# A second MLP's first layer by seven products of quadrants, on one core of a Trainium2 chip

## The chip, the cores and the metric

The kernel runs as one program on one core of one Trainium2 chip. The metric is the device time of one execution in microseconds (us). TensorE does the matrix products, VectorE (DVE in the rows) and ScalarE (ACT) the work between them; SyncE (SP) issues every DMA from one queue.

## What is computed

```python
def _moe_ref(x, w_gate, w_val, w_out, rms_g):
    rms = np.sqrt(np.mean(x * x, axis=-1, keepdims=True) + 1e-06)
    xn = x / rms * rms_g
    g = xn @ w_gate
    silu = g * (1.0 / (1.0 + np.exp(-g)))
    val = xn @ w_val
    return silu * val @ w_out

def _moe2_ref(x, w_in, w_out):
    h = x @ w_in
    g = np.maximum(0.01 * h, h)
    return g @ w_out

def reference(**kwargs):
    attn_out = _attn_ref(...)            # B, H, S, D = 4, 8, 544, 64
    x = attn_out.transpose(0, 2, 1, 3).reshape(B * S, H * D)
    x = _moe_ref(x=x, **moe_kwargs)      # 512 -> 1536 -> 512
    return _moe2_ref(x=x, **moe2_kwargs) # 512 -> 2048 -> 512
```

There are 2176 tokens (4 batches of 512 local and 32 global rows) of 512 columns. The weights of both MLPs come as 64-bit floats.

## The kernel before

Attention and the first MLP (`mlp1`) are not changed, apart from the jobs that `mlp1` carries along for the second MLP. The first MLP leaves its result y, transposed, in DRAM (`y_dram`, four chunks of 128 columns by 2176 tokens).

Every product is made of three matmuls (`mm3`, L69 to L72): each operand is split into a high part in the reduced 32-bit format and the rest (`split`: a cast on ScalarE at L75, a subtraction on VectorE at L78), and high x high, low x high and high x low are added up in PSUM. Each of these matmuls loads its own 128 x 128 weights.

The second MLP goes over token blocks of 512, 512, 512, 384 and 256 (`BLOCKS2`). For each block there are 16 steps f (NF2 = 16 groups of 128 hidden columns). A step makes `ph`, 128 hidden columns by n tokens, out of 4 chunks of the inner dimension, so 12 matmuls of n columns (L820); then leaky ReLU on ScalarE (`tl`, L822) and a split (`h2h`, `h2l`); and then, for the step before, the second layer (`out2_step`, L809): for every 128 tokens 3 matmuls of 512 columns into the banks `o`. PSUM has 4 banks for `ph` and 4 for `o`.

A 64-bit weight tile (128 x 512, 512 KB; `w64b`) becomes a 32-bit one in `weights2`: a DMA, `narrow` (one ScalarE instruction at L99 into `nc_b`, two of VectorE at L101 and L103, `nr_b` and `wfb`), and a split into `w0h`, `w0l` (first layer) or `w1h`, `w1l` (second). There are 32 such tiles, and all 64 halves stay in SBUF for the rest of the program. `ahead` makes 12 of them and the first block's split y while the first MLP's last blocks run; the other 20 are made during block 0 of the second MLP, with three buffers for `w64b`.

The order on every engine is fixed when the program is built: a list scheduler goes by the program's order and by when it expects each instruction's inputs and buffers. On the chip every engine takes its rows strictly in that order, SP's DMA issues included.

Of the kernel before, what the change touches and what calls it, by code (L numbers as in the profile page):

```python
# [20 lines left out]


@with_exitstack
def tile_window_global_attention_two_mlps(
# [600 lines left out]
    def rows_in(i, c, tmp, tag):  # L632

        pool, n, c0 = pre2[0], BLOCKS2[i], sum(BLOCKS2[:i])
        if c == 0:
# [4 lines left out]

    def weights2(f, k, pool, tmp, tag, bufs, wf_bufs):

        r = tmp.tile([P, DM, 2], U32, tag=tag, bufs=bufs, name=f"w64b{k}_{f}")
# [1 line left out]
        wf = tmp.tile([P, DM], F32, tag="wf", bufs=wf_bufs, name=f"wfb{k}_{f}")
        narrow(tmp, wf, r, f"b{k}_{f}")
        w2_s[f, k] = [pool.tile([P, DM], F32R, tag=f"w{k}{y}{f}", name=f"w{k}{y}{f}") for y in "hl"]
        split(w2_s[f, k][0], w2_s[f, k][1], wf)

    def ahead():  # L650

        ph_at.close()
# [1 line left out]
        jobs = []
        for f in range(6):
            for k in range(2):
                jobs.append(lambda f=f, k=k: weights2(f, k, pre2[0], mp, f"w64{k}", W64[k], 7))
        for c in range(KC):
            jobs.insert(2 * (c + 1) - 1, lambda c=c: rows_in(0, c, mp, "sq"))
# [140 lines left out]
    c0 = 0  # L800
    for i, n in enumerate(BLOCKS2):
        if i not in ys2:
            for c in range(KC):
                rows_in(i, c, wp2, "yf")
        ys = ys2.pop(i)
        op = [pools[0].tile([P, DM], F32, tag="y", bufs=4, name=f"o{t}_{i}") for t in range(n // P)]
        pend = None

        def out2_step(f, hs):  # L809
            for t in range(n // P):  # L810
                mm3(op[t], [h[:, t * P:(t + 1) * P] for h in hs], w2_s[f, 1], f == 0, f == NF2 - 1)

        for f in range(NF2):
            if i == 0:
                for k in range(2):
                    if (f, k) not in w2_s:
                        weights2(f, k, wp2, wp2, "w64", 3, 2)
            pp = bank(f"ph{i}_{f}")
            for c in range(KC):
                mm3(pp[:, 0:n], [w[:, c * P:(c + 1) * P] for w in w2_s[f, 0]], [y[:, c, 0:n] for y in ys], c == 0, c == KC - 1)  # L820
            tl = wp2.tile([P, NY], F32, tag="tl", bufs=2, name=f"tl{i}_{f}")
            nc.scalar.activation(out=tl[:, 0:n], in_=pp[:, 0:n], func=AF.Prelu, alpha=0.01)  # L822
            hs = [wp2.tile([P, NY], F32R, tag=f"h2{y}", bufs=2, name=f"h2{y}{i}_{f}")[:, 0:n] for y in "hl"]
            split(hs[0], hs[1], tl[:, 0:n])
            if pend:
                out2_step(*pend)
            pend = (f, hs)
        out2_step(*pend)
        for t in range(n // P):
            ob = wp2.tile([P, DM], F32, tag="ob", bufs=2, name=f"ob{i}_{t}")  # L830
            if t % 2:
                nc.vector.tensor_copy(ob, op[t])
            else:
                nc.scalar.copy(ob, op[t])
            for r0, o, m in rows(c0 + t * P, P):
                nc.sync.dma_start(out=out[r0:r0 + m, :], in_=ob[o:o + m, :])
        c0 += n


# [57 lines left out]
```

## Time and profile before

| what | value |
|---|---|
| three runs, median (lowest to highest) | 978.49 us (978.25 to 978.88) |
| the profiled execution: span from its first to its last instruction | 977.8 us |
| what the runs have around that span, by their median | 0.7 us |
| TensorE matmul busy | 947.7 us of the span (97%), 5280 matmuls |
| VectorE, ScalarE busy | 476.7 us (49%), 429.6 us (44%) |
| mean granted TensorE clock | 0.991 |
| second MLP: first matmul of `ph` to last matmul of `o` | 595.8 us to 972.7 us |

The page gives busy times as shares of the span. Matmuls are pipelined, so that a matmul's duration (0.39 us at 512 columns) is longer than the time from its start to the next one's start; the second is what counts in a sum. The timeline view gives starts; the windows view gives, for a stretch, each engine's busy time, the granted clock and the bytes moved by DMA.

### The profile page before, as it was taken

The numbers are of one execution on the slowest core, as the hardware profiler recorded it, in microseconds if no ns is written. First come the engines' busy times: TensorE is split into PE (matmuls) and PEld (weight loads), VectorE is DVE, ScalarE is ACT, GpSimd is POOL, SyncE is SP. The second block draws the span as 40 slices with busy tenths as digits, with TensorE's granted clock in tenths as the row PEclk, the third lists the DMA queues.
The fourth block names the chain that finished last, engine by engine and source line by source line (L and its number), as shares of the span: only waits on it lengthen the run. The fifth ranks groups of instructions, "written<-read, shape, count | busy, mean of one in ns | idle before, by whom it ended". The sixth has DMA issues, their size and how long they took to land.

```text
span 977.8 us, 14074 instructions
## 1 busy us (share of the span) xinstructions
PE 947.7 (97%) x5280; PEld 785.1 (80%) x5280; DVE 476.7 (49%) x1055; ACT 429.6 (44%) x965; POOL 4.5 (0%) x26
## 2 busy tenths in 40 slices
PE   6799999999999999999999999999999999999998
PEld 4557777777777777778899999878888888889997
DVE  5689985587563664535677542871211211121111
ACT  6886774665443442424555322762222312232232
POOL 1000000000000000000000000000000000000000
PEclk9899999999999999999999999999999999999999
DMA  9587994785767555344798852840200200010000
GB/s 291 180 293 261 332 356 153 250 309 195 288 209 269 195 161 179 109 151 151 249 326 294 269 170 85 288 150 6 75 1 1 70 1 1 0 54 1 1 34 22
DMA packets 60628, 157.16 MB, mean 161 GB/s; under 512 B 9232, under 2 KB 11280, under 8 KB 60560
## 3 DMA queue, kind: packets, MB, share of 16 engines
q1 hardware_dynamic: 60560, 156.27, 47.8%
q8 instruction: 41, 0.67, 0.3%
q14 instruction: 27, 0.22, 0.1%
HBM read 119.02 MB, written 37.22 MB: 160 GB/s over the span
## 4 chain that ended last, share of the span: by engine, by line
PE 76%; DMA 6%; DVE 2%; ACT 2%; issue 1%; SPq 0%; DVEq 0%; ACTq 0%
PE o L72 17%; PE ph L72 17%; PE pg L72 12%; PE yp L72 11%; PE pv L72 11%; DMA w64b<-w 3%; PE po L139 2%; DMA y_dram<-ys 2%; PE sc L139 2%; PE pp L248 1%; PE pz_g L139 1%; DMA w_f<-wf 1%; PE sa_g L139 0%; DMA yf<-y_dram 0%; DVE ys L599 0%
## 5 line engine op out<-in xcount | busy, mean ns | idle before, releaser
L78 DVE TENSOR_TENSOR h2l<-tl,h2h 128x512 fp32r<-128x512 f32 (+2 forms) x80 | 48.8, 611 | 236.0 <-ACT h2h L75 236.0
L72 PE MATMUL pg<-xh,w 128*128 128x512 f32 (+1 forms) x464 | 133.3, 370 | 0.4 <-ACT xh L75 0.4
L72 PE MATMUL pv<-xh,w 128*128 128x512 f32 (+1 forms) x464 | 129.6, 361 | 0.0
L822 ACT ACTIVATE tl<-ph 128x512 f32<-128x512 f32 (+2 forms) x80 | 42.5, 533 | 197.3 <-PE ph L72 197.2
L72 PE MATMUL yp<-hsh,w 128*128 128x512 f32 (+1 forms) x480 | 125.3, 364 | 2.6 <-ACT hsh L75 1.5
L72 PE MATMUL ph<-yspl,w0h 128*128 128x512 f32 (+2 forms) x320 | 114.3, 357 | 0.0
L72 PE MATMUL ph<-ysph,w0l 128*128 128x512 f32 (+2 forms) x320 | 114.3, 357 | 0.0
L72 PE MATMUL ph<-ysph,w0h 128*128 128x512 f32 (+2 forms) x320 | 114.3, 357 | 0.0
L72 PE MATMUL o<-w1h,h2l 128*128 128x512 f32 x272 | 106.5, 392 | 1.1 <-DVE h2l L78 0.9
L72 PE MATMUL o<-w1l,h2h 128*128 128x512 f32 x272 | 106.1, 390 | 0.0
L72 PEld LDWEIGHTS yp<-hsh,w 128*128 128x128 f32 x480 | 84.3, 188 | 15.9 <-ACT hsh L75 2.3
L72 PEld LDWEIGHTS pg<-xh,w 128*128 128x128 f32 x464 | 81.4, 190 | 17.8 <-issue 6.6
L72 PEld LDWEIGHTS pv<-xh,w 128*128 128x128 f32 x464 | 82.5, 189 | 11.5 <-issue 0.9
L72 PE MATMUL pg<-xl,w 128*128 128x512 f32 (+1 forms) x232 | 83.9, 361 | 0.0
L72 PE MATMUL pv<-xl,w 128*128 128x512 f32 (+1 forms) x232 | 83.0, 358 | 0.0
L72 PE MATMUL o<-w1h,h2h 128*128 128x512 f32 x272 | 78.2, 391 | 0.0
L75 ACT CAST w<-wf 128x512 fp32r<-128x512 f32 x92 | 56.6, 617 | 45.5 <-PE yp L72 24.8
L72 PE MATMUL yp<-hsl,w 128*128 128x512 f32 (+1 forms) x240 | 76.4, 362 | 0.0
L228 ACT ACTIVATE s_ring<-s_ring,mx 128x224 f32<-128x224 f32 x128 | 60.2, 472 | 35.4 <-DVE mx L225 35.2
L78 DVE TENSOR_TENSOR w<-wf,w 128x512 fp32r<-128x512 f32 x92 | 63.0, 687 | 22.4 <-ACT w L75 21.9
L72 PEld LDWEIGHTS ph<-ysph,w0h 128*128 128x128 f32 x320 | 60.2, 188 | 8.8
L72 PEld LDWEIGHTS ph<-yspl,w0h 128*128 128x128 f32 x320 | 60.2, 188 | 8.7
(129 smaller groups left out, 1376.5 us busy)
## 6 DMA issues: line engine op xcount, KB each, us to landing
w<-w_dram SPq DMA_DIRECT2D x84, 512.0 KB, 4.3
w<-w SPq DMA_DIRECT2D x36, 512.0 KB, 5.6
w_dram<-w SPq DMA_DIRECT2D x36, 512.0 KB, 3.8
w64b<-w SPq DMA_DIRECT2D x32, 512.0 KB, 6.0
wf<-w_f SPq DMA_DIRECT2D x60, 256.0 KB, 4.4
kq<-kqv SPq DMA_DIRECT2D x32, 352.0 KB, 4.5
w_f<-wf SPq DMA_DIRECT2D x36, 256.0 KB, 5.3
va<-kqv SPq DMA_DIRECT2D x16, 256.0 KB, 5.3
```

The lines of the kernel that those rows point to most:

```text
L72: nc.tensor.matmul(dst, lhs[a], rhs[b], start=first and i == 0, stop=last and i == 2)
L75: nc.scalar.copy(hi, src)
L78: nc.vector.tensor_tensor(out=lo, in0=src, in1=hi.bitcast(F32), op=ALU.subtract)
L139: x = nc.tensor.matmul(dst, lhs, rhs, start=start, stop=stop)
L228: x = nc.scalar.activation(out=sp, in_=sp, func=AF.Exp, bias=mx[:, c:c + 1], scale=-1.0, accum_out=sm[:, c:c + 1])
L248: nc.tensor.transpose(pp[:, n * P:(n + 1) * P], s[:, c0:c0 + P], ident)
L822: nc.scalar.activation(out=tl[:, 0:n], in_=pp[:, 0:n], func=AF.Prelu, alpha=0.01)
```

## The change

The first layer of the second MLP is regarded as a 2 x 2 matrix product of quadrants and done by Strassen's algorithm (in Winograd's form): the inner dimension is halved (chunks 0 and 1, chunks 2 and 3), the hidden columns are halved (steps j and j + 8 form a pair), and a block's tokens are halved. Seven products of quadrants take the place of eight, each of 2 chunks x 3 matmuls of n/2 columns. The sums of weight quadrants (4 subtractions or additions of 128 x 256) and of y quadrants (4 subtractions) are made on VectorE before the splits; the sums of products are made as they leave PSUM: one copy on ScalarE (`x`), and five additions on VectorE (`u`, `v`, and three into `r`), and three of the products are accumulated onto another product's bank. A pair's seven weight sums, high and low, are one tile `wr` of 128 x 3584 words (1.835 MB).

The tiles `wr` do not all stay in SBUF: in block 0 they are made pair by pair, two buffers in turn, and each is written to DRAM (`w2_dram`); the other blocks read them back, three buffers in turn. Only 2 of the 8 pairs and one second-layer tile are made during the first MLP; 12 + 15 = 27 raw tiles `w64b` are left for block 0, with two buffers. The blocks are 640, 512, 512 and 512 tokens, so that products have 320 or 256 columns. PSUM has 3 banks for products and 5 for `o`.

```diff
-BLOCKS2 = [512, 512, 512, 384, 256]
+BLOCKS2 = [640, 512, 512, 512]
...
+    def sums(q):
+        b12, b11, t2, t3, t1, b21, t4, b22 = (q[:, s] for s in range(8))
+        for dst, x, y in ((t1, b12, b11), (t2, b22, t1), (t3, b22, b12), (t4, b21, t2)):
+            nc.vector.tensor_tensor(out=dst, in0=x, in1=y, op=ALU.subtract)
...
-    def weights2(f, k, pool, tmp, tag, bufs, wf_bufs):
+    def weights_in(j, tmp, tag, bufs, nar):
+        q = pre2[0].tile([P, 8, HK], F32, tag="q", name=f"wq{j}")
+        for s, f in ((0, j + PAIRS), (2, j)):
+            r = raw2(f, 0, tmp, tag, bufs)
+            narrow(tmp, q[:, s:s + 2].rearrange("p s c -> p (s c)"), r, f"b0_{f}", nar)
+        a21, a22, a11, a12, s1, s2, s3, s4 = (q[:, s] for s in range(8))
+        for dst, x, y, op in ((s1, a21, a22, ALU.add), (s2, s1, a11, ALU.subtract),
+                              (s3, a11, a21, ALU.subtract), (s4, a12, s2, ALU.subtract)):
+            nc.vector.tensor_tensor(out=dst, in0=x, in1=y, op=op)
+        t = w_in[0, j] = pre2[0].tile([P, 2, 7, HK], F32R, tag="wr", bufs=2, name=f"wr{j}")
+        for r in (slice(0, 3), slice(3, 7)):
+            split(t[:, 0, r], t[:, 1, r], q[:, r.start + 1:r.stop + 1])
+        nc.sync.dma_start(out=w2_dram[j], in_=t.bitcast(F32).rearrange("p y s c -> p y (s c)"))
...
+    def load2(i, j):
+        q = (i - 1) * PAIRS + j
+        pool, tag, bufs = (late[0], "wr3", 1) if q % 3 == 0 else (pre2[0], "wr", 2)
+        t = w_in[i, j] = pool.tile([P, 2, 7, HK], F32R, tag=tag, bufs=bufs, name=f"wr{i}_{j}")
+        nc.sync.dma_start(out=t.bitcast(F32).rearrange("p y s c -> p y (s c)"), in_=w2_dram[j])
...
+    def product(i, j, which, dst, start=True):
+        w, part, s = PRODUCT[which]
+        t, y = w_in[i, j], ys2[i, part]
+        for k in range(KC // 2):
+            mm3(dst, [t[:, h, w, k * P:(k + 1) * P] for h in range(2)], [y[:, h, k, s] for h in range(2)],
+                start and k == 0, k == KC // 2 - 1, not start)
...
+        for j in range(PAIRS):
...
+            product(i, j, 1, b[0])
+            nc.scalar.copy(x1, b[0])
+            product(i, j, 6, b[1])
+            plus(u2, x1, b[1])
+            product(i, j, 7, b[2])
+            plus(v, u2, b[2])
...
+            if pend:
+                out2_step(*pend.pop(0))
+            z = bank(f"pz{i}_{j}")[:, 0:n]
+            product(i, j, 5, z)
+            plus(r[1][:, n:2 * n], v, z)
+            product(i, j, 2, b[0], False)
+            leaky(r[0][:, 0:n], b[0])
+            product(i, j, 4, b[2], False)
+            plus(r[1][:, 0:n], u2, b[2])
+            product(i, j, 3, z, False)
+            plus(r[0][:, n:2 * n], u2, z)
+            leaky(r[0][:, n:2 * n], r[0][:, n:2 * n])
+            h = [halves2(i, j, r[0], n)]
+            leaky(r[1], r[1])
+            h.append(halves2(i, j + PAIRS, r[1], n))
+            if pend:
+                out2_step(*pend.pop(0))
...
+            if i == 0:
+                if j + 2 < PAIRS:
+                    weights_in(j + 2, prep, "w64", 2, 1)
+                for f in (j + PAIRS, j + 1) if j < PAIRS - 2 else (NF2 - 2, j + 1, NF2 - 1):
+                    if f not in w_out:
+                        weights_out(f, wp2, prep, "w64", 2, 1, 1)
```

How the order moves is shown at three places of block 0. Line numbers in the rows of the change are those of the changed kernel.

On SP, the issues of block 0 before: raw weight tiles (`w64b`), with y between them.

```order
L644 DMA w64b_9_6538<-w 128x1024
L644 DMA w64b_10_6581<-w 128x1024
L638 DMA yf_0_7467<-y_dram 128x512
L644 DMA w64b_10_6593<-w 128x1024
L638 DMA yf_1_7471<-y_dram 128x512
```

On SP, the same place now, around the pair j = 5 (`wr_6686` is its tile of weight sums, `w_dram_105` the DRAM tile that it goes to).

```order
L662 DMA w64b_14_6822<-w 128x1024
L678 DMA w_dram_105<-wr_6686 128x3584
L662 DMA w64b_6_6829<-w 128x1024
L662 DMA w64b_12_6846<-w 128x1024
L662 DMA w64b_5_6858<-w 128x1024
L662 DMA w64b_15_6967<-w 128x1024
L678 DMA w_dram_106<-wr_6840 128x3584
```

There was no store among the raw loads; now each step has one of 1.835 MB, and the raw tile that the next pair needs last (`w64b_6`) stands right behind it.

On VectorE before, a piece of block 0: conversions (`nr_b`, `wfb`, `w0l`, `w1l`) and one `h2l` for each step f.

```order
L101 TENSOR_SCALAR nr_b_10_6585<-w64b_10_6581 128x512
L103 SCALAR_TENSOR_TENSOR wfb_9_6540<-nc_b_9_6541,nr_b_9_6542 128x512
L78 TENSOR_TENSOR w0l_6535<-wfb_9_6528,w0h_6534 128x512
L78 TENSOR_TENSOR h2l_5_6346<-tl_5_6343,h2h_5_6345 128x512
L101 TENSOR_SCALAR nr_b_10_6597<-w64b_10_6593 128x512
```

On VectorE now, from the arrival of `w64b_6` to the end of pair 6's tile `wr_6840`: L871 are sums that read PSUM (`pz`, `py`), L674 the sums of weight quadrants in `wq`.

```order
L104 TENSOR_SCALAR nr_b_6_6832<-w64b_6_6829 128x512
L106 SCALAR_TENSOR_TENSOR wq_6821<-nc_b_6_6831,nr_b_6_6832 128x512
L871 TENSOR_TENSOR r_13_6874<-v_5_6877,pz_5_6914 128x320
L674 TENSOR_TENSOR wq_6821<-wq_6821 128x256 x2
L104 TENSOR_SCALAR nr_b_12_6850<-w64b_12_6846 128x512
L871 TENSOR_TENSOR r_13_6874<-u_5_6876,py_5_6872 128x320
L674 TENSOR_TENSOR wq_6821<-wq_6821 128x256
L81 TENSOR_TENSOR wr_6840<-wq_6821,wr_6840 128x768
L106 SCALAR_TENSOR_TENSOR wfb_12_6848<-nc_b_12_6849,nr_b_12_6850 128x512
L871 TENSOR_TENSOR r_5_6873<-u_5_6876,pz_5_6914 128x320
L81 TENSOR_TENSOR wr_6840<-wq_6821,wr_6840 128x1024
```

What leaves PSUM for pair 5 and what is made for pair 6 now stand in one row of instructions, each behind the one above.

On VectorE now, the first rows of block 0, behind the first MLP's last copies (`ys`).

```order
L602 COPY ys_3_6138<-yp_3_5523 128x320
L871 TENSOR_TENSOR u_0_6158<-x_0_6157,pw_0_6153 128x320
L871 TENSOR_TENSOR v_0_6159<-u_0_6158,py_0_6154 128x320
L104 TENSOR_SCALAR nr_b_10_6227<-w64b_10_6224 128x512
L871 TENSOR_TENSOR r_8_6156<-v_0_6159,pz_0_6181 128x320
```

The sum `r_8` has to read `pz_0` before the next product is accumulated onto it, and it now stands behind the first raw tile of block 0.

## Rows read from the trace of the kernel before

**Rows 1.** The page: busy us (share of the span) and count of each engine.

```profile
PE 947.7 (97%) x5280; PEld 785.1 (80%) x5280; DVE 476.7 (49%) x1055; ACT 429.6 (44%) x965; POOL 4.5 (0%) x26
```

**Rows 2.** Windows, second MLP: us, busy PE, PEld, DVE, ACT, POOL (count), clock, DMA share, GB/s.

```profile
595.80:689.50 93.70, 92.59 (x410) 75.75 (x409) 49.17 (x87) 47.74 (x84) 0.00 (x0) 1.00 0.45 144
689.50:778.00 88.50, 88.50 (x392) 73.26 (x392) 15.15 (x23) 23.02 (x39) 0.00 (x0) 1.00 0.07 23
```

**Rows 3.** Timeline, PE: start us, us, instruction, count.

```profile
585.24 0.46 PE L72 MATMUL pg<-xh,w 128*128 128x320 f32 x2
590.52 0.46 PE L72 MATMUL pg<-xh,w 128*128 128x320 f32 x2
595.80 0.39 PE L72 MATMUL ph<-ysph,w0h 128*128 128x512 f32 x1
684.33 0.39 PE L72 MATMUL ph<-ysph,w0l 128*128 128x512 f32 x1
687.73 0.39 PE L72 MATMUL ph<-ysph,w0l 128*128 128x512 f32 x1
872.47 0.33 PE L72 MATMUL ph<-ysph,w0h 128*128 128x384 f32 x1
874.23 0.33 PE L72 MATMUL ph<-ysph,w0l 128*128 128x384 f32 x1
926.44 0.28 PE L72 MATMUL ph<-yspl,w0h 128*128 128x256 f32 x1
927.87 0.28 PE L72 MATMUL ph<-yspl,w0h 128*128 128x256 f32 x1
972.71 0.39 PE L72 MATMUL o<-w1l,h2h 128*128 128x512 f32 x1
```

**Rows 4.** Groups by form, DVE: count, busy us, mean ns, idle before.

```profile
L101 DVE TENSOR_SCALAR nr_b<-w64b 128x512 uint32<-128x512 uint32 x32 | 13.6, 424 | 9.2 <-DMA w64b<-w 9.2
L103 DVE SCALAR_TENSOR_TENSOR wfb<-nc_b,nr_b 128x512 uint32<-128x512 uint32 x32 | 22.0, 687 | 1.0 <-ACT nc_b L99 0.6
L737 DVE SCALAR_TENSOR_TENSOR th<-th,pv 128x320 f32<-128x320 f32 x24 | 11.6, 485 | 7.1 <-PE pv L72 6.7
L238 DVE TENSOR_TENSOR s_ring<-s_ring,sm 128x896 f32<-128x896 f32 x32 | 34.9, 1090 | 0.8
```

**Rows 5.** Timeline, DVE, at block 0's start and in its conversions: [idle <-releaser].

```profile
603.06 0.49 DVE L599 COPY ys<-yp 128x320 f32<-128x320 f32 x1 [2.04 <-DMA y_dram<-ys]
631.37 0.43 DVE L101 TENSOR_SCALAR nr_b<-w64b 128x512 uint32<-128x512 uint32 x1
631.71 0.69 DVE L103 SCALAR_TENSOR_TENSOR wfb<-nc_b,nr_b 128x512 uint32<-128x512 uint32 x1
632.31 0.69 DVE L78 TENSOR_TENSOR w1l<-wfb,w1h 128x512 fp32r<-128x512 f32 x1
```

**Rows 6.** Groups by form, ACT.

```profile
L99 ACT ACTIVATE nc_b<-w64b 128x512 f32<-128x512 f32 x32 | 21.6, 676 | 10.1 <-DMA w64b<-w 10.0
```

**Rows 7.** Tile view of `w64b`, and DMA issues: KB each, median us to landing.

```profile
DMA to landing us min/median/max: 4.2/6.0/8.3
y_dram<-ys SPq DMA_DIRECT2D x8, 160.0 KB, 2.3
```

**Rows 8.** Windows, where DMA is busiest (columns as rows 2).

```profile
476.00:479.00 3.00, 3.00 (x22) 3.00 (x21) 1.08 (x3) 0.99 (x4) 0.00 (x0) 1.00 1.03 415
611.00:626.00 15.00, 15.00 (x68) 12.43 (x67) 12.51 (x24) 11.43 (x21) 0.00 (x0) 1.00 0.91 298
```

**Rows 9.** Windows and waits around TensorE's one wait of 2 us.

```profile
479.00:481.40 2.40, 0.47 (x4) 0.21 (x2) 2.40 (x6) 1.84 (x7) 0.00 (x0) 1.00 0.78 277
481.40:485.60 4.20, 4.14 (x16) 3.99 (x17) 2.90 (x3) 3.98 (x6) 0.00 (x0) 0.61 0.66 205
PE pm L455 <- DVE ssum L448: 2.0, 1, 2.0
```

**Rows 10.** The page, costliest groups: weight loads of `ph`.

```profile
L72 PEld LDWEIGHTS ph<-ysph,w0h 128*128 128x128 f32 x320 | 60.2, 188 | 8.8
```

More of the change, by code (lines that the diff above doesn't have):

```diff
@@ L60, in tile_window_global_attention_two_mlps @@
     w1_f32 = [[dram.tile([P, DM], F32, name=f"w1_f32{k}_{f}") for k in range(3)] for f in range(NF1)]
+    HK = KC // 2 * P
+    w2_dram = [dram.tile([P, 2, 7 * HK], F32, name=f"w2_dram{j}") for j in range(NF2 // 2)]
     w1_dram = [[dram.tile([P, 2, DM], F32, name=f"w1_dram{k}_{f}") for k in range(3)] for f in range(NF1)]
@@ L67, in tile_window_global_attention_two_mlps, with mm3 @@
     mm3_order = ((0, 0), (1, 0), (0, 1))
-    def mm3(dst, lhs, rhs, first=True, last=True):
+    def mm3(dst, lhs, rhs, first=True, last=True, onto=False):
         for i, (a, b) in enumerate(mm3_order):
-            nc.tensor.matmul(dst, lhs[a], rhs[b], start=first and i == 0, stop=last and i == 2)
+            nc.tensor.matmul(dst, lhs[a], rhs[b], start=first and i == 0, stop=last and i == 2,
+                             skip_group_check=onto)
     def high(hi, src):
@@ new lines, in quads_in, with operands @@
+    def quads_in(q, c0, n, k, d, w):
+        for s, kc, half in ((0, k, 1), (1, k, 0), (5, k + KC // 2, 0), (7, k + KC // 2, 1)):
+            c = c0 + half * n + d
+            nc.sync.dma_start(out=q[:, s, :], in_=y_dram[:, kc, c:c + w])
+    def operands(i, part, quads, d, w):
+        n = BLOCKS2[i] // 2
+        lo_slot, m = ((1, 3), (4, 4))["ab".index(part)]
+        if (i, part) not in ys2:
+            ys2[i, part] = pre2[0].tile([P, 2, KC // 2, m, n], F32R, tag="ys" + part, name=f"ys{part}{i}",
+                                        padded_shape=[P, 2, KC // 2, m, NH])
+        t = ys2[i, part]
+        for k, q in quads:
+            split(t[:, 0, k, :, d:d + w], t[:, 1, k, :, d:d + w], q[:, lo_slot:lo_slot + m])
@@ L643, in weights2, with raw2 @@
+    def raw2(f, k, tmp, tag, bufs):
         r = tmp.tile([P, DM, 2], U32, tag=tag, bufs=bufs, name=f"w64b{k}_{f}")
         nc.sync.dma_start(out=r, in_=words(w2[f])[:, k])
[L645 to L648, printed above, removed]
+        return r
+    def weights_in(j, tmp, tag, bufs, nar):
[11 more added lines that the diff above has]
+        nc.sync.dma_start(out=w2_dram[j], in_=t.bitcast(F32).rearrange("p y s c -> p y (s c)"))
@@ L650, in ahead, with weights_out @@
+    def weights_out(f, pool, tmp, tag, bufs, nar, wf_bufs):
+        r = raw2(f, 1, tmp, tag, bufs)
+        wf = tmp.tile([P, DM], F32, tag="wf", bufs=wf_bufs, name=f"wfb1_{f}")
+        narrow(tmp, wf, r, f"b1_{f}", nar)
+        w_out[f] = [pool.tile([P, DM], F32R, tag=f"w1{y}{f}", name=f"w1{y}{f}") for y in "hl"]
+        split(w_out[f][0], w_out[f][1], wf)
     def ahead():
@@ L653, in ahead, with rows_in @@
         pre2.append(ctx.enter_context(tc.tile_pool(name="pre2", bufs=1, side="right", reuse_waits="tile")))
[L654 to L659, printed above, removed]
+        n = BLOCKS2[0] // 2
+        def rows_in(k, d):
+            q = pre2[0].tile([P, 8, n // 2], F32, tag="q", name=f"yq0_{k}_{d}", padded_shape=[P, 8, HK])
+            quads_in(q, 0, n, k, d, n // 2)
+            sums(q)
+            for part in "ab":
+                operands(0, part, [(k, q)], d, n // 2)
+        jobs = [lambda j=j: weights_in(j, mp, "w640", W64[0], 2) for j in range(2)]
+        jobs[1:1] = [lambda k=k, d=d: rows_in(k, d) for k in range(KC // 2) for d in (0, n // 2)]
+        jobs.append(lambda: weights_out(0, pre2[0], mp, "w641", W64[1], 2, 7))
         return jobs
@@ L796, in tile_window_global_attention_two_mlps @@
     ph1.close()
+    ph_ps.close()
+    pools[:] = ctx.enter_context(tc.tile_pool(name="ps2", bufs=1, space=PSUM, reuse_waits="tile")), 3
     wp2 = ctx.enter_context(tc.tile_pool(name="wp2", bufs=1, reuse_waits="tile"))
[L800 to L813, printed above, removed]
-            if i == 0:
[L815 to L832, printed above, removed]
-            else:
[L834 to L837, printed above, removed]
@@ new lines, in leaky, with half_sum, out2_step @@
+    def leaky(out, x):
+        nc.scalar.activation(out=out, in_=x, func=AF.Prelu, alpha=0.01)
+    def half_sum(what, i, j, n):
+        return wp2.tile([P, NH], F32, tag=what, name=f"{what}{i}_{j}")[:, 0:n]
+    def out2_step(i, f, h, op):
+        for t in range(BLOCKS2[i] // P):
+            mm3(op[t], [h[:, y, t * P:(t + 1) * P] for y in range(2)], w_out[f], f == 0, f == NF2 - 1)
+            if f == NF2 - 1:
+                ob = wp2.tile([P, NY], F32, tag="r", bufs=3, name=f"ob{i}_{t}")[:, 0:DM]
+                if t % 2:
+                    nc.vector.tensor_copy(ob, op[t])
+                else:
+                    nc.scalar.copy(ob, op[t])
+                for r0, o, m in rows(sum(BLOCKS2[:i]) + t * P, P):
+                    nc.sync.dma_start(out=out[r0:r0 + m, :], in_=ob[o:o + m, :])
@@ new lines, in halves2 @@
+    def halves2(i, f, r, n):
+        h = wp2.tile([P, 2, NY], F32R, tag="h2", bufs=3, name=f"h2_{i}_{f}")
+        split(h[:, 0, 0:2 * n], h[:, 1, 0:2 * n], r)
+        return h
+    pend, quads = [], []
+    for i, n2 in enumerate(BLOCKS2):
+        n = n2 // 2
+        more = i + 1 < len(BLOCKS2)
+        op = None
+        for j in range(PAIRS):
+            b = [bank(f"p{c}{i}_{j}")[:, 0:n] for c in "xwy"]
+            r = [wp2.tile([P, NY], F32, tag="r", bufs=3, name=f"r{i}_{f}")[:, 0:2 * n] for f in (j, j + PAIRS)]
+            x1, u2, v = (half_sum(w, i, j, n) for w in ("x1", "u2", "v"))
+            product(i, j, 1, b[0])
[4 more added lines that the diff above has]
+            plus(v, u2, b[2])
+            if j == PAIRS - 1 and more:
+                operands(i + 1, "a", quads, 0, BLOCKS2[i + 1] // 2)
+            if pend:
[15 more added lines that the diff above has]
+                out2_step(*pend.pop(0))
+            if op is None:
+                op = [pools[0].tile([P, DM], F32, tag="y", bufs=5, name=f"o{t}_{i}") for t in range(n2 // P)]
+            pend = [(i, f, x, op) for f, x in zip((j, j + PAIRS), h)]
+            if i == 0:
+                if j + 2 < PAIRS:
[3 more added lines that the diff above has]
+                        weights_out(f, wp2, prep, "w64", 2, 1, 1)
+                if j == PAIRS - 2:
+                    ph_prep.close()
+                    late.append(ctx.enter_context(tc.tile_pool(name="late", bufs=1, reuse_waits="tile")))
+                    load2(1, 0)
+                    load2(1, 1)
+                elif j == PAIRS - 1:
+                    load2(1, 2)
+            else:
+                load2(*divmod((i * PAIRS + j) + 3, PAIRS))
+            if more and 2 <= j < 2 + KC // 2:
+                m = BLOCKS2[i + 1] // 2
+                q = wp2.tile([P, 8, m], F32, tag=f"q{j}", name=f"yq{i + 1}_{j}")
+                quads_in(q, sum(BLOCKS2[:i + 1]), m, j - 2, 0, m)
+                sums(q)
+                quads = [x for x in quads if j > 2] + [(j - 2, q)]
+            if j == PAIRS - 1 and more:
+                operands(i + 1, "b", quads, 0, BLOCKS2[i + 1] // 2)
@@ L841 @@
+    for x in pend:
+        out2_step(*x)
 def kernel(q_l, k_l, v_l, q_g, k_g, v_g, moe_w_gate, moe_w_val, moe_w_out, moe_rms_g, moe2_w_in, moe2_w_out):
```

30 lines of the change are left out of this document (17 added, 13 removed).

## The prediction

> **What bounds the kernel now.** I read the page first. TensorE's matmuls are busy in 947.7 of 977.8 us; VectorE and ScalarE in about half [rows 1]. So a saving has to come from TensorE, and other engines count only where they come to stand in its way. The windows over the second MLP show the same: in block 0, where 20 raw weight tiles are converted, PE is busy 92.59 of 93.70 us with VectorE at 49.17, and in the next stretch 88.50 of 88.50 with VectorE at 15.15 [rows 2].
>
> Then the timeline of PE, for what a matmul costs in a row of matmuls, from start to start [rows 3]. 320 columns: 590.52 − 585.24 = 5.28 us for 36 matmuls, 0.1467 each. 512: 3.40 us for 15, 0.2267. 384: 1.76 for 10, 0.176. 256: 1.43 for 12, 0.119.
>
> By these, the second MLP now needs: first layer 576 x 0.2267 (three blocks, 16 steps, 12 matmuls) + 192 x 0.176 + 192 x 0.119 = 187.3 us; second layer 17 token tiles x 48 = 816 x 0.2267 = 185.0; together 372.3. It took 972.71 + 0.23 − 595.80 = 377.1, in which 12 matmuls of the first MLP (1.76) still lie [rows 3], so 375.4. The 3.1 us between are waits: nearly all of the second MLP is PE at its pace.
>
> **The change part by part.**
>
> *Products.* Seven products of 2 chunks x 3 matmuls, 8 pairs: 336 per block, in place of 192 of double width. 336 x 0.1467 (320 columns) + 1008 x 0.119 (256 columns) = 49.3 + 120.0 = 169.3 us, **18.0 less**. The second layer keeps its 816 matmuls. The order holds 1344 and 816, so the change does on TensorE what it says. The waits of before, 3.1, stand at places that no longer exist: **−3.1**, and what replaces them is counted below.
>
> The Trainium skill speaks against this: "TensorE: Matmul & The Clock Gate", section "Back-to-back issue gap", gives 81 ns for a matmul of 128 columns and 131 ns for 512 in a sustained stream of loads and matmuls, so width hardly pays. By a straight line between the two, an estimate, the first layer would be 116 us before and 134 after, 18 us more in place of 18 less. The trace disagrees: it has 0.119 at 256 and 0.2267 at 512 [rows 3], near to proportional.
>
> *Block 0, what one pair's step needs.* PE: 42 x 0.1467 + 30 x 0.2267 (five token tiles, two steps f) = 12.96 us. VectorE: an instruction in a row starts about 0.09 us before the one ahead has its full duration: nr_b goes at 0.34, one of 512 columns at 0.60 [rows 5]. From 426 ns at 256, 485 at 320 and 1090 at 896 columns [rows 4], less 0.085: 0.34, 0.40, and on the line between 512 and 896: 0.735 at 640, 0.87 at 768, 1.14 at 1024. A pair's weights are 2 x (0.34 + 0.60) + 4 x 0.34 + 0.87 + 1.14 = 5.25; two second-layer tiles 2 x (0.34 + 0.60 + 0.60) = 3.08; the sums out of PSUM 5 x 0.40 and the two low halves 2 x 0.735 = 3.47. In all 11.8, so VectorE just fits, and 13.8 by full durations. DMA: four raw tiles of 0.524 MB and a store of 1.835 = 3.93 MB a step.
>
> *Block 0, the loop that I think decides.* The order on SP puts the raw tile that the next pair needs last right behind the store of this pair's `wr`, and the store waits for the last low half of `wr`. When the raw tile has landed, 12 rows of VectorE (shown in the order) lead to the next `wr`'s last low half: nr_b, wq, a sum, two quadrant sums, nr_b, a sum, a quadrant sum, 768, wfb, a sum, 1024 = 0.34 + 0.60 + 0.40 + 0.68 + 0.34 + 0.40 + 0.34 + 0.87 + 0.60 + 0.40 + 1.14 = 6.1. `wq` needs ScalarE's nc_b first, 0.676 [rows 6] against nr_b's 0.34: +0.34; and 0.15 from engine to engine: 6.6. So the period of a step is the landing L of store and tile together, plus 6.6. The store itself is not shown in the trace. I bound L: a transfer of 160 KB lands after 2.3 us, some 1.9 without its own bytes [rows 7]; 2.36 MB at 415 GB/s, where the DMA engines are full, is 5.7 us, and at the 298 GB/s of the stretch of conversions 7.9 [rows 8]. So 7.6 to 9.8; without a store, a raw tile needs 4.2 to 8.3, median 6.0 [rows 7]. I take 8.1, near the lower end, since the row of 415 also has large tiles one behind the other. 8.1 + 6.6 = 14.7 against PE's 12.96: 1.74 for each of 5 steps (pairs 2 to 7 follow on one another), 8.7, and 0.8 for one step whose fifth product stands behind 15 second-layer matmuls: **+9.5**. Bounds: 0, were the store out of the way of the tile, and 18.
>
> *Start of block 0.* PE ends the first MLP at 595.80 + 1.76 = 597.6 [rows 3]. Before, VectorE's copy of the last y waits 2.04 us for a store [rows 5]. Now the first sums `u_0` and `v_0` stand behind that copy, and the raw loads are issued behind the stores of y, at about 601.5; with 4.8 to landing (range 4.2 to 8.3 [rows 7]) the first comes at 606.3. `r_8`, which frees `pz_0` for the next product, stands behind its nr_b, so PE waits from 603.8 to about 607. Then 26 rows of VectorE, 12.1 us, lead to the low half that pair 2 needs, at about 618.8; PE has work for 17.2 us, to 614.8: **+4.0**, the wait at 607 included. Bounds: 1.3 with an early raw tile, 7.5 with one at 8.3.
>
> *End of block 0.* Behind the last store PE has 22.1 us of work; block 1's first tile of weights is read back into memory that the conversions held, behind two more tiles, about 25.0 after that store: **+2.9**, between 0 and 5.
>
> *Blocks 1 to 3.* PE needs 42 x 0.119 + 24 x 0.2267 = 10.4 us a step, VectorE and ScalarE less than half, and reading back 1.835 MB in it is 175 GB/s, under the 298 and 415 of [rows 8]; so it is hidden. At each of three boundaries the y sums and halves come in a burst: 0.5 each, **+1.5**, between 0 and 4.
>
> *Clock.* Around TensorE's one wait of 2.0 us the granted clock fell: PE is idle in most of 479.0 to 481.4, and then has 0.61, with 16 matmuls in 4.2 us [rows 9], where the stretch before had 22 in 3.0 [rows 8], so some 28 to 30 were due: about 1.8 us lost. 1.2 and 2.4 GHz are its two levels. The change has one such wait at the start (part of which is hidden behind the wait for `wr`, 1.3 left) and waits of 1.7 in the steps, where I count 1.2: **+2.5**, between 0 and 10.8 (one drop in each of six steps).
>
> *Sum*, against the median of 978.5 (the profiled span of 977.8 and 0.7 around it): 978.5 − 18.0 − 3.1 + 4.0 + 9.5 + 2.9 + 1.5 + 2.5 = **977.8**. A measurement of this kernel can tell about 0.2%, 2 us, from no change; this is inside. What TensorE saves is spent by block 0's loop.
>
> **The rivals.**
>
> *B, faster.* The loop keeps to PE's step: VectorE's 11.8 lies under 12.96, and 3.93 MB in 12.96 us is 303 GB/s, between the rows' 298 and 415. This needs the tile to land within 12.96 − 6.6 = 6.4 us of the store's issue; the tile alone has that (6.0), so it happens if the transfers share the engines rather than follow one another. Against it: 2.36 MB in 6.4 less 1.9 would be 524 GB/s. Then 9.5 goes, and the clock's part in the steps: 977.8 − 10.7 = 967. Chance 0.24.
>
> *C, slower.* Block 0 falls further behind: at L = 9.8 a step is 16.4 and five cost 8.5 more, 986; if each step's wait then drops the clock as in [rows 9], up to 1.8 a step and 7 to 8 more, 994. It decides from L over about 9, for which the 298 GB/s of block 0's own row speaks [rows 8]. Against it: in that stretch the DMA engines were 0.91 busy, with pauses. I put it at 990. Chance 0.26.
>
> *D, narrow matmuls do not go faster.* If each matmul of the products took as long as a weight load, 188 ns [rows 10], 1344 would need 252.7 us, 83 more than in my sum, and block 0's loop and the clock's part would be hidden: 1,046. Matmuls of 256 columns with their own loads ran at 0.119 [rows 3], so 0.02. The rule of the Trainium skill above is this rival's milder form.
>
> **How the numbers follow.** The forecast has 0.48; its own range is 971 to 984 (L 7.6 without a drop of the clock or boundary cost; or the start and end at their upper bounds), of which 0.19 lie below −0.2%, 0.17 within and 0.12 above. Faster: 0.24 + 0.19 = 0.43. Same 0.17. Slower: 0.26 + 0.12 + 0.02 = 0.40. Signs on both sides hold most of the chance. The range from 964 to 992 leaves out the far end of B (0.05), of C (0.06) and D.
>
> **What the profile of the changed kernel would show.** First, starts 0.147 and 0.119 apart in the products; anything over 0.13 at 256 columns is D. Second, in block 0, from 597.6 to about 718 by this sum (103.7 of PE work and some 16 of waits), PE waiting for VectorE's `wr` once a step, and VectorE for the DMA of `w64b`, with a period near 14.7; 13.0 with no such wait is B, 16 or more C. Third, the landing of raw tiles behind a store at 8 us, others nearer 6. Fourth, the granted clock in block 0 under 1 in one or two stretches, and 1.00 from block 1 on, with PE busy all through. Wrong would also be a wait in blocks 1 to 3 for the tiles read back, or block 0's loop bound by VectorE at 13.8 with DMA long done.

## The result

The changed kernel takes 990.62 us (median of 4 runs, 988.71 to 994.19) against 978.68: ratio 1.0135, 95% interval 1.0115 to 1.0155. It is slower, by about 12 us, where the forecast was no change (977.8). The profiled execution is the one of 988.71 us.

### The profile after

The page: the same two lines as [rows 1], and the span.

```profile
span 986.9 us, 15204 instructions
PE 937.9 (95%) x5664; PEld 792.6 (80%) x5664; DVE 571.0 (58%) x1271; ACT 449.7 (46%) x997; POOL 4.5 (0%) x26
```

TensorE does less (937.9 for 947.7 us busy) and yet ends later: the time in which it does nothing grew from 30 to 49 us. Where, the timeline of PE tells with the waits. First the pace: the first product of pair 0, the first products of block 1, and the last matmul.

```profile
593.75 1.04 PE L74 MATMUL px<-ysa,wr 128*128 128x320 f32 x6
...
720.61 0.88 PE L74 MATMUL px<-ysa,wr 128*128 128x256 f32 x6
721.33 0.88 PE L74 MATMUL pw<-ysa,wr 128*128 128x256 f32 x6
...
980.29 0.39 PE L74 MATMUL o<-w1l,h 128*128 128x512 f32 x1
```

Six matmuls of 256 columns in 0.72 us: 0.12 each, as [rows 3] had it. In this execution the second MLP starts at 593.75, not at 597.6, and block 0 runs to 720.6. Next the waits of PE, from 590 us to the end (total, times, longest).

```profile
PE pz L74 <- DVE r L871: 6.4, 4, 3.3
PE o L74 <- ACT h L78: 5.5, 2, 3.9
PE px L74 <- DVE wr L81: 3.9, 3, 1.3
PE pw L74 <- DVE wr L81: 1.7, 2, 0.8
PE pz L74 <- DVE ysb L81: 0.9, 2, 0.5
PE py L74 <- DVE r L871: 0.9, 1, 0.9
PE pw L74 <- ACT wr L78: 0.7, 1, 0.7
```

20.0 us of waits: for a sum out of PSUM (`r`), for the second layer's operand (`h`), for weight sums (`wr`). Windows over the stretches behind the waits add the clock (us, PE busy, PEld, DVE, ACT, POOL, clock, DMA share, GB/s).

```profile
602.87:608.00 5.13, 5.13 (x24) 5.13 (x25) 4.62 (x12) 3.99 (x8) 0.00 (x0) 0.67 0.89 283
...
628.00:707.10 79.10, 71.89 (x377) 61.67 (x375) 62.60 (x117) 44.77 (x74) 0.00 (x0) 1.00 0.78 275
707.10:710.95 3.85, 0.01 (x1) 0.01 (x1) 3.49 (x6) 3.85 (x7) 0.00 (x0) 0.87 0.78 315
710.95:716.97 6.02, 6.02 (x15) 4.71 (x16) 3.39 (x7) 0.57 (x1) 0.00 (x0) 0.51 0.98 333
...
735.20:980.50 245.30, 239.60 (x1484) 214.98 (x1482) 88.81 (x180) 76.66 (x152) 0.00 (x0) 1.00 0.46 165
```

The pairs' steps lose time at full clock (628 to 707); after the waits of 3.3 and 3.9 us the clock is at 0.67 and 0.51 for 5 to 6 us; blocks 1 to 3 still have 5.7 us of idle PE. What is late there, the chain of waits shows (start, us, what).

```profile
631.74 8.16 DMA w64b<-w
...
661.35 8.50 DMA w64b<-w
...
692.54 11.63 DMA w64b<-w
...
707.51 1.88 ACT ysb L78 x2
...
729.61 7.12 DMA out<-ob
...
802.23 7.14 DMA wr<-w_dram
809.38 4.04 DMA yq<-y_dram
...
900.29 8.33 DMA out<-ob
```

In block 0 a raw tile of 512 KB takes 8 us right behind a store of 1.8 MB, 11.6 us at the end, where a reload stands ahead of it too (SP's timeline).

```profile
687.79 0.33 SPq L857 DMA_DIRECT2D wr<-w_dram  x1
...
711.58 0.36 SPq L857 DMA_DIRECT2D wr<-w_dram  x1
```

Behind blocks 0 and 2 it is an output that takes 7 or 8 us behind a reload; without one ahead outputs landed in about 2 us. Behind block 1 the chain goes through a reload and a y tile that waits for it. At the first of these boundaries the late output holds a buffer that ScalarE's next copy needs, and VectorE's sum `r` then waits 6.2 us for that copy. ScalarE's wait:

```profile
ACT ob L887 <- DMA out<-ob: 6.6, 1, 6.6
```

Put beside the sum, term by term. "Lost" is here what the starts of PE's matmuls in the timeline lie further apart than at the paces 0.1467, 0.2267 and 0.119 of the prediction, so it counts waits, restarts and slow clock alike.

| term | forecast | profiled execution |
|---|---|---|
| products | −18.0 | −18.0 |
| waits of the second MLP before | −3.1 | −3.1 |
| first MLP ends sooner | not seen | −3.8 |
| start of block 0, with its clock | +5.3 | +5.4 |
| steps of block 0, with their clock | +10.7 | +10.4 |
| end of block 0 | +2.9 | +6.8 |
| blocks 1 to 3 | +1.5 | +7.4 |
| pace of the second layer | 0 | +2.4 |
| behind the last matmul, and around the span | 0 | +2.6 |
| sum from 978.5 | 977.8 | 988.6 |

Two rows need care. Of the 7.4 in blocks 1 to 3, waits are 5.7, and about 0.5 is the products' own pace there (0.1195 for 0.119). And the −3.8 compares one execution with one: see the section on the first MLP.

### The profile page after: what moved, and what is told of

The parts are those of the page before. It is cut to its first block, busy times and chain, and to the rows that moved or that the text cites. A ratio compares the mean times of both kernels' runs of the same rounds, so it can differ in the third digit from the quotient of the medians.

```text
span 986.9 us, 15204 instructions
## 1 busy us (share of the span) xinstructions
PE 937.9 (95%) x5664; PEld 792.6 (80%) x5664; DVE 571.0 (58%) x1271; ACT 449.7 (46%) x997; POOL 4.5 (0%) x26
## 4 chain that ended last, share of the span: by engine, by line
PE 64%; DMA 12%; DVE 5%; ACT 4%; issue 1%; SPq 1%; DVEq 0%; ACTq 0%
PE o L74 14%; PE pg L74 10%; PE yp L74 10%; PE pv L74 10%; DMA w64b<-w 5%; PE px L74 4%; PE pz L74 4%; PE py L74 3%; DMA yq<-y_dram 2%; PE po L142 2%; DMA out<-ob 2%; PE pw L74 2%; PE sc L142 2%; DMA y_dram<-ys 1%; PE pp L251 1%
## 5 line engine op out<-in xcount | busy, mean ns | idle before, releaser
L74 PE MATMUL o<-w1h,h 128*128 128x512 f32 x544 | 168.3, 397 | 5.5 <-ACT h L78 5.5
L74 PEld LDWEIGHTS o<-w1h,h 128*128 128x128 f32 x544 | 101.1, 191 | 24.2 <-ACT h L78 6.1
L74 PE MATMUL o<-w1l,h 128*128 128x512 f32 x272 | 100.0, 395 | 0.0
L874 ACT ACTIVATE r<-r 128x512 f32<-128x512 f32 (+1 forms) x64 | 34.7, 544 | 86.2 <-DVE r L871 86.2
L74 PE MATMUL pz<-ysb,wr 128*128 128x256 f32 (+1 forms) x384 | 60.4, 291 | 7.4 <-DVE r L871 6.4
L74 PEld LDWEIGHTS pz<-ysb,wr 128*128 128x128 f32 x384 | 54.7, 190 | 11.8 <-DVE r L871 8.2
L74 PEld LDWEIGHTS o<-w1l,h 128*128 128x128 f32 x272 | 51.4, 190 | 10.0 <-DVE w1l L81 0.4
L78 ACT CAST hsh<-th 128x512 fp32r<-128x512 f32 (+1 forms) x60 | 33.4, 556 | 54.1 <-DVE th L781 53.3
L781 DVE SCALAR_TENSOR_TENSOR th<-th,pv 128x512 f32<-128x512 f32 (+1 forms) x60 | 36.3, 605 | 30.0 <-PE pv L74 29.3
L81 DVE TENSOR_TENSOR h<-r,h 128x512 fp32r<-128x512 f32 (+1 forms) x64 | 44.8, 720 | 13.7 <-ACT h L78 13.7
```

Source lines behind the costliest of these rows:

```text
L781: nc.vector.scalar_tensor_tensor(out=t, in0=t, scalar=0.5, in1=pp[1][:, 0:n], op0=ALU.mult, op1=ALU.mult)
L874: nc.scalar.activation(out=out, in_=x, func=AF.Prelu, alpha=0.01)
```

## The experiments

### Is it the queue?

Theories on record: Q, the big transfers delay what stands behind them in SyncE's one queue; E, the DMA engines' bandwidth is short, whatever the queue; S, the row of instructions on VectorE. Three runs moved the big transfers to GpSimd's own queue.

**e1_reload_queue**

```diff
-        nc.sync.dma_start(out=t.bitcast(F32).rearrange("p y s c -> p y (s c)"), in_=w2_dram[j])
+        nc.gpsimd.dma_start(out=t.bitcast(F32).rearrange("p y s c -> p y (s c)"), in_=w2_dram[j])
```

> The 24 reloads of wr (1.835 MB each) are issued by GpSimd from its own DMA queue; everything else stays on SyncE's. Theory Q (transfers wait for the big one ahead of them in SyncE's queue): the last raw tiles of block 0, landing after 10.4 and 11.6 us in the changed kernel, land in 5 to 8 again, the outputs of a block in 2 to 3 us in place of 7 to 8; the wait for h at 707 us (3.9), the slow clock behind it (2.8) and the waits behind blocks 0 to 2 (5.5) go for the most part; time 8 to 12 us below the changed kernel, 979 to 983; block 0's loop keeps its period of 15 us. Rival E (the 16 engines' bandwidth is what is short, whatever the queue): landings and time within 2 us of the changed kernel, 988 to 993. Rival S (the schedule: sums of products stand in the row of VectorE behind conversions): the wait for h stays at 3 us or more.

Measured: 991.22 us, ratio to the kernel before 1.0140 (1.0123 to 1.0157). Nothing gained. From the chain, at block 0's end:

```profile
695.46 11.18 DMA w64b<-w
```

and from the tile view of `ob`, at the first boundary:

```profile
DMA to landing us min/median/max: 2.0/6.6/7.6
```

A late raw tile still took 11.2 us, and outputs up to 7.6. Here a queue of their own did not get small transfers past a large one: Q falls in this form. The time lies in E's band, and PE's wait for `h` is still 3.8 us, which is S's sign, so this run leaves both standing.

**e2_store_queue**

```diff
-        nc.sync.dma_start(out=w2_dram[j], in_=t.bitcast(F32).rearrange("p y s c -> p y (s c)"))
+        nc.gpsimd.dma_start(out=w2_dram[j], in_=t.bitcast(F32).rearrange("p y s c -> p y (s c)"))
```

> The 8 stores of wr are issued from GpSimd's queue; reloads and all else stay on SyncE's. Theory Q: the raw tile that stood behind the store lands in 5 to 6 us in place of 8.2, the period of block 0's loop falls from 15.0 to PE's 13.0, five waits of 1 to 3 us go: 8 to 10 us less, 980 to 983. Rival E: the store takes its share of the engines all the same, the tile lands at about 8, the period stays over 14.5, time 988 to 992.

Measured: 997.61 us, 1.0213 (1.0194 to 1.0232), 7 us slower than the changed kernel and above both bands. The steps keep their waits for `wr` (3.5 and 1.7 us). Most of the loss is in the first MLP, where the pair 0 store goes out at 499.55; the chain there,

```profile
500.70 9.88 DMA yq<-y_dram
```

and PE's waits:

```profile
PE yp L74 <- DVE hsl L81: 4.5, 1, 4.5
```

The y tile itself was not slower than before: in the changed kernel's chain it takes 9.69 us there, issued on SP right behind the store, and PE has no such wait. What differs is the place of VectorE's row on it. In the changed kernel `hsl` runs ahead of it:

```profile
503.02 0.49 DVE L81 TENSOR_TENSOR hsl<-th,hsh 128x320 fp32r<-128x320 f32 x1 [0.53 <-ACT hsh L78]
...
510.84 0.33 DVE L640 TENSOR_TENSOR yq<-yq 128x160 f32<-128x160 f32 x1 [3.82 <-DMA yq<-y_dram]
```

In e2 it runs behind it, and PE needs it:

```profile
510.68 0.33 DVE L640 TENSOR_TENSOR yq<-yq 128x160 f32<-128x160 f32 x1 [7.97 <-DMA yq<-y_dram]
510.93 0.48 DVE L81 TENSOR_TENSOR hsl<-th,hsh 128x320 fp32r<-128x320 f32 x1
```

So the edit moved more than the queue: with the store gone from SP, the fixed order on VectorE came out otherwise, and e2 is no clean measure of a second queue.

**e3_both_queues** (both lines)

> Stores and reloads of wr both from GpSimd's queue. Theory Q: the two gains add up, 16 to 22 us less, 969 to 975, so faster than the kernel before. Rival E: 986 to 992.

Measured: 998.36 us, 1.0208 (1.0181 to 1.0235). The two do not add up to a gain; the time is above both bands, and the first MLP has e2's wait for `hsl` again (4.4 us).

### Is it the place in the order?

So I formed theory O: a transfer has to wait for the bytes that were issued ahead of it, on whichever queue; what can be changed is what is issued ahead. Three edits, alone and together.

**e5_three_raw**

```diff
-                    weights_in(j + 2, prep, "w64", 2, 1)
+                    weights_in(j + 2, prep, "w64", 3, 1)
...
-                        weights_out(f, wp2, prep, "w64", 2, 1, 1)
+                        weights_out(f, wp2, prep, "w64", 3, 1, 1)
```

On SP now, beside the order shown ahead: the tile that the next pair needs stands ahead of the store.

```
L662 DMA w64b_14_6822<-w 128x1024
L662 DMA w64b_6_6829<-w 128x1024
L678 DMA w_dram_105<-wr_6686 128x3584
L662 DMA w64b_12_6846<-w 128x1024
```

> Three buffers for w64b in block 0 in place of two. On SyncE the raw tile that the next pair needs (w64b_5, w64b_6, w64b_7) now stands ahead of the store of wr instead of behind it; nothing else moves there. Theory O (what counts is the place in the order: the tile waits for the bytes that were issued ahead of it, on whichever queue): the store is out of the loop, a tile lands 4 to 6 us after its issue, the period falls from 15.0 us to PE's 13.0 and the 10.4 us lost in the steps fall to 2 or less; 8 to 10 us below the changed kernel, 980 to 983. Rival E (the engines' bandwidth, 3.93 MB a step): the period stays at 14.5 to 15, 988 to 992. Rival V (VectorE's row, 11.8 to 13.8 a step): the period falls to 13.8 at most, 984 to 987.

Measured: 978.13 us, 0.9989 (0.9969 to 1.0009): the kernel before's time, 12 us below the changed kernel. The stores on SP's timeline, of the changed kernel (second and last of the six in block 0),

```profile
631.31 0.33 SPq L678 DMA_DIRECT2D w_dram<-wr  x1
...
691.29 0.33 SPq L678 DMA_DIRECT2D w_dram<-wr  x1
```

and of this one:

```profile
633.98 0.33 SPq L678 DMA_DIRECT2D w_dram<-wr  x1
...
686.98 0.33 SPq L678 DMA_DIRECT2D w_dram<-wr  x1
```

On average, four periods of 15.0 us (14.35 to 15.6) became four of 13.25 (13.0 to 13.6); the interval ahead of these, 16.15 us, became 14.2. PE has no wait at all between 613 and 702 us. The same bytes and the same work of VectorE go through in 13.25 us a step, so neither E nor V bound the steps. A tile issued behind the store still takes 8.4 us, but it is one that nobody on the path waits for. The profiled execution is the longest of the ten (983.58): its block 0 starts at 598.49, and from there to the end it is 9.8 us shorter than the changed kernel's, close to the 10.4 lost in the steps. Where the other 2 of the 12 us come from is not shown.

**e12_order_alone**: the same with two buffers.

```diff
             r = raw2(f, 0, tmp, tag, bufs)
+            if f == j and stores:
+                with tc.issue_after(anchors["raw"]):
+                    stores.pop()()
...
+        if 2 <= j < PAIRS - 1:
+            stores.append(store)
```

> Two buffers for w64b as in the changed kernel, but the store of wr is issued behind the raw tile that the next pair needs instead of ahead of it. Theory O (the place in the order alone): the tile lands after 4 to 5 us in place of 8.2, the period falls to 13.0 to 13.5, the 10.4 us lost in the steps fall to 3 or less; 978 to 983, as with three buffers. Rival P (it was the third buffer, so that tiles are fetched sooner): with two the tile has to wait for its buffer, the store slides back too and delays the tiles behind it; a period of 14 to 15, 985 to 990.

Measured: 990.17 us, 1.0129 (1.0103 to 1.0154). The period is 14.2 us, and PE's waits in the steps are short:

```profile
PE px L74 <- ACT x L913: 1.3, 3, 0.7
PE pw L74 <- DVE wr L81: 0.4, 2, 0.2
```

Those behind them, up to 735 us:

```profile
PE px L74 <- DMA wr<-w_dram: 4.8, 1, 4.8
PE o L74 <- ACT w1h L78: 4.8, 2, 4.0
```

Half of the steps' loss goes (10.4 to 4.7) by the order alone; the other half went only with the third buffer. The whole gain is lost at the end of block 0, where the last raw tiles and block 1's first reload now come later, and the time is the changed kernel's again. My number was a miss, and the rival's band held the time, for another reason than the one it gave.

**e6_reload_late**

```diff
-                    load2(1, 0)
-                    load2(1, 1)
+                    with tc.issue_after(anchors["raw"]):
+                        load2(1, 0)
+                        load2(1, 1)
```

> The first two reloads of wr for block 1 are issued behind the last raw tile of block 0; the order is otherwise the same. Theory O: the last two raw tiles, landing after 10.4 and 11.6 us, land in 6 to 9; the wait for h at 707 us (3.9) falls to 1 or less, and the slow clock behind it (2.8 us) goes with it; 4 to 6 us less, 984 to 987. Rival S (the row of VectorE and ScalarE at the end of block 0, ysb and the conversions ahead of h): the wait stays at 3 or more, 988 to 992.

Measured: 987.19 us, 1.0069 (1.0043 to 1.0095). Raw tiles land in at most 8.7 us, the wait for `h` is 1.5 in place of 3.9, and the clock behind it stays at 1.00. The time is just above theory O's band, and S's sign, a wait of 3 or more, did not come:

```profile
709.90:716.00 6.10, 5.83 (x25) 4.80 (x26) 2.01 (x3) 0.85 (x2) 0.00 (x0) 1.00 1.02 432
```

**e7_own_out_buffers**

```diff
-                ob = wp2.tile([P, NY], F32, tag="r", bufs=3, name=f"ob{i}_{t}")[:, 0:DM]
+                ob = wp2.tile([P, DM], F32, tag="ob", bufs=2, name=f"ob{i}_{t}")
```

> The output copies ob get two buffers of their own instead of sharing three with the sums r. Theory B (the waits of 0.9 to 1.9 us behind blocks 0 to 2 come from outputs that land late behind a reload and so hold the buffers that r needs): these waits, 5.5 us with their neighbours, fall to 2 or less; 3 to 4 us less, 986 to 988. Rival (the waits come from the y halves of the next block): no change, 988 to 992.

Measured: 987.03 us, 1.0070 (1.0050 to 1.0091). All five outputs of block 0 are now issued ahead of the reload and land in 2.0 to 3.0 us; from 719 us to the end PE's waits shrink to this one line.

```profile
PE o L74 <- ACT h L78: 0.2, 1, 0.2
```

**e8_all_three** (e5, e6 and e7 together)

> The three edits of the runs before together. Theory O with B: their gains add up, 15 to 20 us below the changed kernel, 971 to 976, faster than the kernel before. If only the order at block 0's end counts, 984 to 987; if nothing of it does, 988 to 992.

Measured: 971.09 us, 0.9905 (0.9881 to 0.9929), faster than the kernel before. In the steps of block 0 PE is busy throughout, with the DMA engines at 0.82:

```profile
628.00:702.00 74.00, 73.97 (x404) 66.11 (x403) 67.49 (x126) 47.70 (x78) 0.00 (x0) 1.00 0.82 288
```

Two waits, of 3.6 and 3.0 us, are left, at the two ends of block 0.

### The two ends of block 0

**e9_sum_first** (on top of e8)

```diff
+            with tc.issue_after(anchors["sum5"]) if j == 2 else nullcontext():
-            narrow(tmp, q[:, s:s + 2].rearrange("p s c -> p (s c)"), r, f"b0_{f}", nar)
+                narrow(tmp, q[:, s:s + 2].rearrange("p s c -> p (s c)"), r, f"b0_{f}", nar)
```

> On top of the run with all three edits: at block 0's start the conversions of the third pair's first raw tiles (nr_b and what follows) stand behind the sum r_8 that frees pz. Theory: the wait of 3.6 us for r at 603 us and the slow clock behind it (2.7) came from that place in VectorE's row alone; the wait falls under 1 us, and as block 0's steps then have no other wait, 4 to 6 us come off the 971: 965 to 967. Rival (the time comes back at the third pair's wr, which hangs on the same raw tiles): a wait of 2 us or more for wr near 630 us, 969 to 972.

Measured: 970.31 us, 0.9912 (0.9892 to 0.9932). The sum `r_8` now runs at 600 us, but the wait only moves, to the leaky ReLU of another product, which on ScalarE stands behind `nc_b` of the same raw tile (timeline of ScalarE):

```profile
603.47 0.69 ACT L102 ACTIVATE nc_b<-w64b 128x512 f32<-128x512 f32 x1 [5.55 <-DMA w64b<-w]
604.04 0.44 ACT L875 ACTIVATE r<-px 128x320 f32<-128x320 f32 x1
```

PE's wait:

```profile
PE px L74 <- ACT r L875: 2.8, 1, 2.8
```

A miss: it was not VectorE's row alone. The time is in the rival's band, but no wait for `wr` came. Both rows have the raw tile ahead of something that PE needs.

**e10_h_first** (on top of e8)

```diff
-                operands(i + 1, "b", quads, 0, BLOCKS2[i + 1] // 2)
+                with tc.issue_after(anchors["h_high"]) if i == 0 else nullcontext():
+                    operands(i + 1, "b", quads, 0, BLOCKS2[i + 1] // 2)
```

> On top of the run with all three edits: at block 0's end the y halves ysb of block 1 stand behind the last h on ScalarE and VectorE. Theory: PE's wait of 3.0 us for h falls to 1.5 or less, with it the 1.4 us of slow clock; 1 to 3 us less than 971, 968 to 970. Rival (the wait is that of the last product's chain: sum, leaky, h): 2.5 us or more stay, 970 to 972.

Measured: 967.93 us, 0.9889 (0.9873 to 0.9904). PE's wait there went from 3.0 to 1.6 us, what the last product's own chain needs. Against e8 the ratio falls by 0.0016, which is inside both intervals: the shorter wait is shown, a gain in time is not.

```profile
697.23 0.47 ACT L874 ACTIVATE r<-r 128x320 f32<-128x320 f32 x1 [2.06 <-DVE r L871]
697.73 1.35 ACT L78 CAST h<-r 128x640 fp32r<-128x640 f32 x2
698.99 1.99 ACT L78 CAST ysb<-yq 128x1024 fp32r<-128x1024 f32 x2
```

**e11_both_firsts** (e9 and e10 together)

> Both edits on top of the three: 963 to 966 if both theories hold, 969 to 972 if neither does.

Measured: 967.85 us, 0.9886 (0.9869 to 0.9903), between what was expected of both and of neither; no better than e10 alone, as e9's wait only moves.

### The first MLP

The changed kernel's first MLP ends 3.8 us sooner in the profiled executions. In the windows of [rows 9] PE now has 29 matmuls at full clock where it had 16 at 0.61:

```profile
481.40:485.60 4.20, 4.20 (x29) 4.04 (x28) 3.08 (x5) 2.65 (x4) 0.00 (x0) 1.00 0.43 95
```

**e4_before_8_ahead**: the kernel before, with fewer conversions in the first MLP.

```diff
-        for f in range(6):
+        for f in range(4):
             for k in range(2):
```

> The kernel before with 8 in place of 12 second-MLP weight tiles converted during the first MLP. Theory: the changed kernel's first MLP ended 3.8 us sooner because no conversion stands among the sums ssum of the last norm, so that PE does not wait 2.0 us there and its clock does not fall; here none stands there either, so the first MLP's last yp ends 3 to 4 us sooner, and the time is 974.5 to 976.5 if the 24 tiles left for block 0 cost it nothing. Rival (the earlier end has to do with the y blocks or the PSUM banks, not with the conversions): no change there, 978 to 981.

Measured: 976.85 us over runs from 974.00 to 979.61, ratio 0.9988 (0.9973 to 1.0003): not told apart from no change. Its profiled execution (974.42 us) has no wait for `ssum`, and the same stretch at full clock:

```profile
481.40:485.60 4.20, 4.20 (x31) 4.20 (x30) 3.31 (x5) 2.90 (x5) 0.00 (x0) 1.00 0.48 154
```

The place of the wait is confirmed by the two traces; what it is worth in the time stays open. For the start of block 0 also moves with no change ahead of it: from 593.65 (e6) to 598.49 (e5), two kernels with the first MLP of the changed one and no wait for `ssum`. A difference of 3.8 between two executions lies within that.

## Why the prediction was wrong

**What held.** The products cost what the sum said: 0.12 and 0.147 from start to start, so the width pays nearly in proportion. That is against the rule of the Trainium skill, "TensorE: Matmul & The Clock Gate", section "Back-to-back issue gap", that the prediction weighed. The start of block 0 cost 5.4 for 5.3, nearly all of it in the first of the two waits named (`r_8` behind `nr_b_10`) and the slow clock behind it; the second, for pair 2's `wr`, came to 1.4 and is counted with the steps. The loop through the store was right in place and size: in the four steps from 631.31 on, L, from the store's issue to the tile's landing, was 7.9 to 9.0 for 8.1 (the first: 631.31 to 639.90), and the way from there to the next store 6.4 to 6.9 for 6.6 (in which 0.15 from engine to engine has no row behind it), so a period of 15.0 for 14.7. That both totals fit so closely is in part luck: the start's 5.3 held 0.8 for pair 2's `wr`, which came with the steps instead, and the steps' 10.7 held 1.2 for a slow clock that did not come (1.00 from 628 to 707). e5 takes the store out of that loop and the steps' loss goes to nothing, which is rival B's condition met; with the rest as it was, that gives 978 and not B's 967.

**What failed.** First, and largest, the step on blocks 1 to 3: "reading back 1.835 MB in it is 175 GB/s, under the 298 and 415; so it is hidden", with 0.5 at each boundary. The mean rate is hidden; what the sum left out is what a single reload does to the small transfers behind it. At two of the three boundaries outputs took 7 to 8 us for 2, and, sharing three buffers with the sums `r`, at the first kept ScalarE waiting 6.6 us and VectorE behind it; PE lost 7.4 us in all. e7, which only separates the buffers and with that issues the outputs first, gets PE through these blocks with one wait of 0.2. What was to be seen there, PE busy all through from block 1 on, is what the profile contradicts.

Second the end of block 0, +2.9 for a late reload. The reload that the forecast meant, of block 1's first tile, was late indeed: issued at 711.58 and 8.2 us in landing, it was there 28.5 us behind the last store, for 25.0. But PE was later still and did not wait for it. What held PE up is another reload, by its place that of the second pair's tile, which the sum did not count against the raw tiles: it went out early, at 687.79, ahead of the last raw tiles, so that the last but one landed after 11.6 us. VectorE and ScalarE came to the last product's sums late, with `ysb` ahead of `h` on top: 3.9 us of wait and 2.9 of slow clock. e6 and e10 show both parts. In e12, where the last raw tile and with it block 1's first tile come later still, PE does wait for that tile (4.8).

Third, two things that the sum put at nothing: the second layer's matmuls at 0.228 to 0.232 instead of 0.2267, and 2.6 us behind the last matmul and around the span; 1.1 of these are time around the span (1.8 for 0.7), and the kernel before has 1.8 there too in the later rounds. One thing went the other way in the profiled execution, the 3.8 us of the first MLP.

**Rival C** named 990, and the time is 990.6, but not by its mechanism: L was 7.9 to 9.1 in the steps where C counted with 9.8, and their clock did not fall (1.00 from 628 to 707). Its number is chance.

## What to carry to other kernels

A mean rate under what the DMA engines can move does not say that a transfer issued right behind a large one is hidden: for each small transfer on the path, read in the order which bytes stand ahead of it, and add their time. A second queue was no help here; another buffer, or a reload issued later, was. And where one engine's row has work for a late tile ahead of work that frees PSUM, moving it on that engine alone moves the wait to the next engine with the same tile.

## What the runs showed that I had not expected

- Moving one transfer to another queue also moved the fixed order on another engine: a y tile that landed no later than before held PE up for 4.5 us, because `hsl` now stood behind VectorE's row on it (e2).
- The length of a wait alone does not tell whether the clock falls. Windows behind the wait at block 0's start: after 2.2 us (e11) the clock was at 0.68,

```profile
604.40:609.00 4.60, 4.43 (x21) 4.44 (x22) 3.83 (x10) 4.12 (x9) 0.00 (x0) 0.68 0.99 356
```

after 3.6 us (e8) at 0.50,

```profile
607.40:613.00 5.60, 5.48 (x20) 5.48 (x21) 4.13 (x11) 3.42 (x7) 0.00 (x0) 0.50 1.03 379
```

and after 3.0 us (e10) it stayed at 1.00:

```profile
603.36:608.50 5.14, 4.99 (x34) 5.00 (x35) 4.98 (x14) 4.21 (x9) 0.00 (x0) 1.00 1.01 362
```

  So the price of a wait has to leave room for 0 to nearly 3 us on top.
- Second-layer matmuls of 512 columns, unchanged, ran at 0.229 among products of 256 (chain of the changed kernel: 12 in 2.75 us) and at 0.2267 among first-layer ones of 512 [rows 3]. What the 1% comes from was not tried.

```profile
751.00 2.75 PE o L74 x12
```
